# One decoder block for one token: the last rows of the down projection as whole rows, the first keys in one load, and two engines that copy wo's rows

## The chip, the cores and the metric

The kernel runs on one core of a Trainium2 chip. The metric is the device time of one execution in microseconds, the median of several runs. The core has TensorE (matmuls), VectorE, ScalarE, GpSimd and SyncE; each engine works through its own instructions in order and waits for others on semaphores. Data comes from the chip's memory through 16 DMA engines, here nearly all of it by transfers that SyncE issues one after the other on one queue.

## The reference

A block with adaptive layer norm, for a single token of width 640, against a key and value cache of 32 heads x 16384 positions x 128, in bf16:

```python
mod = (_silu(c) @ w_mod).reshape(c.shape[0], 6, 1, -1)
sa, ca, ga, sb, cb, gb = ...
h = _layernorm(x) * (1 + ca) + sa
x = x + ga * attention(h)          # q = h @ wq; softmax(q k^T / sqrt(128)) v for 32 heads; then @ wo
h = _layernorm(x) * (1 + cb) + sb
x = x + gb * ((_silu(h @ w_gate) * (h @ w_up)) @ w_down)      # 640 -> 1728 -> 640
```

Keys and values are 134 MB each; all weights together are 22 MB.

## The kernel before

The 32 heads are worked in 16 pairs. A pair's keys (8.39 MB) are one load into half of the buffer `kring`, its values one load into `vbuf`; the last pair's values go into the other half of `kring`. Each partition holds 256 positions of one of the two heads.

For a pair, VectorE multiplies the keys by the query (mult) and adds halves of the 128 products together (fold), in place, until 16 are left. TensorE adds these 16 with an identity matrix into `S_ps` (R). Then VectorE takes the largest score (pm, nb), ScalarE the exponentials (exp), TensorE the product with the values (pv), and a diagonal is picked out (diag). Pairs 1 to 14 cut the work by columns in `step` (L554, L559, L564, L544), in a loop; pairs 0 and 15 cut it by positions in `score_end` and `reduce_end` (L570, L576, L584), two halves each, by `KCUT`. Pair p's step also does the rest of pair p - 1.

The order of SyncE's loads is written out by hand, and each waits for the buffer that it overwrites. At the start: w_mod, wq, pair 0's keys, pair 1's keys (after mod_mm1, the last reader of w_mod in that half of `kring`), pair 0's values (after the last query matmul, as wq lies in `vbuf`). Then, for each p from 1: the keys of pair p + 1 wait for R of pair p - 1 (`o_R[p - 2]` in `load_k`), the values of pair p for pv of pair p - 1 (`o_pv[p - 1]` in `load_v`). The line of every DMA is L90, that of the helper.

After pair 15's scores the weights of the rest follow on the same queue: wo in two loads after pv14, and w_gate, w_up and w_down in five loads (`DOWN`) after R15. The tail is a chain of small steps: the attention's output A_sb; wo0 and wo28 (L687), 64 matmuls on 32 columns of the array each, four at a time, with 512 and 128 of the 640 outputs in two PSUM banks; the copies of these to `wo_row` on ScalarE (L693); wo_cols (L699); layer norm; gate and up (L724); the gated vector `gu_col` (L754); the down matmuls (L771), 32 columns of the array each and a quarter of the 640 outputs; the product with gb and the sum with x; the store.

F is 1728 = 13 x 128 + 64, so `gu_col` has 14 columns of which the last counts in its upper 64 partitions only. Before the change, the last 64 rows of w_down lie as 128 half rows on 128 partitions, and their factors are spread to match: twice_gu (a matmul with `twice`) repeats each of the 64 factors, gu_half masks them with `even`.

Of the kernel before, what the change touches and what calls it, by code (L numbers as in the profile page):

```python
# [6 lines left out]
BF16 = mybir.dt.bfloat16  # L7
F32 = mybir.dt.float32
ALU = mybir.AluOpType
ACTF = mybir.ActivationFunctionType  # L10
AX = mybir.AxisListType
# [26 lines left out]
class _Plan:  # L38
# [38 lines left out]
    def op(self, eng, fn, deps=(), name="", chan=None):  # L77
        o = _Op(eng, fn, list(deps), name, len(self.ops), self.loop.get(eng), chan)
        o.sig = chan is not None
        self.ops.append(o)  # L80
        return o
# [137 lines left out]
def build(nc, A_x, A_k, A_v, A_wq, A_wo, B_wg, B_wu, B_wd, c_in, w_mod, out):  # L219
    H, S, Dh = A_k.shape[1], A_k.shape[2], A_k.shape[3]  # L220
    D = A_x.shape[2]
    F = B_wg.shape[1]
# [3 lines left out]
    T2 = 2 * S // 128  # L226
# [4 lines left out]
    NF = 13  # L231
# [3 lines left out]
    DOWN = [(0, 0, 4), (1, 0, 4), (2, 0, 4), (3, 0, 1), (None, 0, 0)]  # L235
    FCH = NF + 1
    QW = 32
    QR = 16
    RW = D // 4
# [3 lines left out]
    with es:  # L243
        block = es.enter_context(nc.Block())
        plan = _Plan(nc, es)
        op, dma = plan.op, plan.dma
        POOL, ACT, DVE, PE = "pool", "act", "dve", "pe"

        def sb(name, shape, dtype):
            return es.enter_context(nc.sbuf_tensor(name, list(shape), dtype))  # L250
# [4 lines left out]
        kb = kring[:, 1].rearrange("p t d -> p (t d)")  # L255
# [5 lines left out]
        wu_v = kb[:, KC * F:2 * KC * F].rearrange("p (k n) -> p k n", k=KC)  # L261
        wd0 = 2 * KC * F
        wd_v = kb[:, wd0:wd0 + NF * D].rearrange("p (k n) -> p k n", k=NF)
        wt_v = kb[:, wd0 + NF * D:wd0 + NF * D + D // 2]

        qbc = sb("qbc", [128, NP, 128], BF16)
        PZ = sb("PZ", [128, NCH, 8], BF16)
# [1 line left out]
        ident = sb("ident", [128, 128], BF16)  # L269
# [41 lines left out]
        rg = sb("rg", [128, FCH], F32)  # L311
        sg = sb("sg", [128, FCH], F32)
        gu_col = sb("gu_col", [128, FCH], BF16)
        gu_half = sb("gu_half", [128, 2], BF16)
        even = sb("even", [128, 2], F32)
        twice = sb("twice", [128, 64, 2], BF16)
        o_row = sb("o_row", [128, RW], BF16)
        gb_row = sb("gb_row", [128, RW], F32)
        ind = sb("ind", [128, 1], F32)
# [2 lines left out]
        wo_row = q_f[:, 0:2 * D].bitcast(F32)  # L322
# [11 lines left out]
        wr_ps = [psb[1], psb[6]]  # L334
        cx_ps = psb[4]
        A_ps = psb[6]
        attn_ps = psb[7]
# [22 lines left out]
        o_ident = op(POOL, lambda e: e.affine_select(  # L360
            out=ident[:], in_=ones_bf[:], pattern=[[1, 128]], compare_op=ALU.is_equal,
            fill=0.0, base=0, channel_multiplier=-1), deps=[o_onesb], name="ident")
# [26 lines left out]
        def layernorm_ops(src_f32, src_dep, sum_ap, c0, tag, xc_t, free=None, between=None):  # L389
# [26 lines left out]
            out=sel[:], in_=ident[:].rearrange("p (s r) -> p r s", s=4)[:, 0:8, :], axis=AX.X, op=ALU.add), deps=[o_ident], name="sel")  # L416
        o_msk = op(DVE, lambda e: e.tensor_reduce(
            out=msk[:], in_=ident[:].rearrange("p (j k) -> p j k", k=32), axis=AX.X, op=ALU.add), deps=[o_ident], name="msk")

        def f_e32(e):  # L420
            with nc.allow_low_precision(reason="sum of one 1 and zeros"):
                return e.tensor_reduce(out=e32[:], in_=ident[:].rearrange("p (j k) -> p k j", k=32), axis=AX.X, op=ALU.add)
        o_e32 = op(DVE, f_e32, deps=[o_ident], name="e32")
        o_even = op(DVE, lambda e: e.tensor_reduce(
            out=even[:], in_=ident[:].rearrange("p (j k) -> p k j", k=2), axis=AX.X, op=ALU.add), deps=[o_ident], name="even")
        o_twice = op(DVE, lambda e: e.tensor_copy(out=twice[64:128], in_=ident[64:128, 64:128].unsqueeze(2).broadcast_to([64, 64, 2])), deps=[o_ident], name="twice")
        o_ind = op(DVE, lambda e: e.tensor_copy(out=ind[:], in_=e32[:, 0:1]), deps=[o_e32], name="ind")


# [14 lines left out]
        def pick(half, n, o_m, free):  # L444
# [13 lines left out]
            out=tt1[:], in0=modc[:, KC:2 * KC], scalar=1.0, in1=xn[:], op0=ALU.add, op1=ALU.mult),  # L458
            deps=[o_m0, o_xn], name="t1")
# [11 lines left out]
        for g in range(H // 4):  # L471
            b = g % 2
# [9 lines left out]
            for half in range(2):  # L482
                ps = slice(64 * half, 64 * half + 64)
                ev.append(op(ACT, lambda e, g=g, b=b, half=half, ps=ps: e.activation(
                    out=qbc[ps, 2 * g:2 * g + 2, :],
                    in_=q_ps[b][ps, :].rearrange("p (a h d) -> p a h d", a=2, h=2)[:, :, half, :], func=ACTF.Copy),
                    deps=[o_q[g]], name="qbc%d_%d" % (g, half)))
# [5 lines left out]
        o_R, o_pv, o_exp, o_nb, o_mx, o_acc, o_ot = ([None] * NP for _ in range(7))  # L493
        KCUT = [0, T2 // 2, T2]
# [2 lines left out]

        def load_k(p):
            deps = [o_R[p - 2]] if p >= 2 else ([o_mod[1]] if p == 1 else [])
            cuts = KCUT if p == 0 else [0, T2]  # L500
            d_k[p] = [dma(kring[:, p % 2, a:b], k_src(p)[:, a:b], ("k", p % 2, c), deps=deps, name="dma_k%d_%d" % (p, c))
                      for c, (a, b) in enumerate(zip(cuts, cuts[1:]))]

# [129 lines left out]
        PL = NP - 1  # L633
# [8 lines left out]
        f1 = score_end(PL, 1)  # L642
# [10 lines left out]
        d_wd = []  # L653
        for i, (b, r0, r1) in enumerate(DOWN):
            if b is None:
                dst, src = wt_v, B_wd[NF * 128:F, :].rearrange("q (h n) -> (q h) n", h=2)
            else:
                f0, n, j0 = BLOCKS[b]
                dst, src = wd_v[:, j0 + r0:j0 + r1, :], B_wd[f0:f0 + 128 * n, :].rearrange("(p r) n -> p r n", r=n)[:, r0:r1, :]
            d_wd.append(dma(dst, src, ("wd", i), deps=wdeps, name="dma_wd%d" % i))  # L660
# [4 lines left out]
                 deps=[o_exp[PL], o_rz, o_onesf, o_rstd], name="L")  # L665
# [5 lines left out]
            out=Z[:].rearrange("p (h j) -> p h j", j=4), in0=msk[:].unsqueeze(1).broadcast_to([128, H, 4]),  # L671
            in1=on_f[:].unsqueeze(2).broadcast_to([128, H, 4]), op=ALU.mult), deps=[o_on, o_msk], name="z")
        o_am = op(PE, lambda e: e.matmul(A_ps[:, 0:H], lhsT=Z[:], rhs=e32[:], start=True, stop=True),
                  deps=[o_z, o_e32] + o_qev[-2], name="am")
# [3 lines left out]
            out=Z[:].rearrange("p (j k) -> p j k", k=32), in_=msk[:].unsqueeze(2).broadcast_to([128, 4, 32])), deps=[o_msk, o_am], name="strips")  # L678

        def project(c):  # L680

            def f_wo(e):
                last = None
                for k in range(WCUT[c], WCUT[c + 1]):
                    r = k % 4
                    for ps, a, b in ((wr_ps[0], 0, 512), (wr_ps[1], 512, D)):
                        last = e.matmul(ps[32 * r:32 * r + 32, 0:b - a], lhsT=wide(A_sb[:, k:k + 1]), rhs=wo_v[:, k, a:b],  # L687
                                        start=(k < 4), stop=(k >= H - 4), tile_position=(0, 32 * r))
                return last
            return op(PE, f_wo, deps=[o_as, d_wo[c], o_exp[NP - 2]] + o_qev[-1], name="wo%d" % c)  # L690
        for c in range(len(WCUT) - 1):
            o_p = project(c)
        o_wr = [op(ACT, lambda e, a=a, b=b, ps=ps: e.activation(out=wo_row[:, a:b], in_=ps[:, 0:b - a], func=ACTF.Copy),  # L693
                   deps=[o_p, f1], name="wo_row%d" % a) for ps, a, b in ((wr_ps[0], 0, 512), (wr_ps[1], 512, D))]

        def f_cols(e):
            last = None
# [9 lines left out]
        o_abf = op(DVE, lambda e: e.tensor_copy(out=attn_bf[:], in_=attn_ps[:, 0:KC]), deps=[o_wo], name="attn_bf")  # L707
        o_ga = op(DVE, lambda e: e.tensor_tensor(out=tt2[:], in0=attn_bf[:], in1=ga, op=ALU.mult), deps=[o_abf, o_m0], name="ga_attn")
        o_x1 = op(DVE, lambda e: e.scalar_tensor_tensor(
            out=x1[:], in0=tt2[:], scalar=1.0, in1=x_f32[:], op0=ALU.mult, op1=ALU.add, accum_out=st[:, 4:5]),  # L710
            deps=[o_ga, o_xf], name="x1")
# [18 lines left out]
        def gate0(o_xc1):  # L730
# [6 lines left out]
            deps=[o_xc1, o_rstd1, o_onep_b], name="t2")  # L737
# [14 lines left out]
        o_sg = op(DVE, lambda e: e.tensor_tensor(out=sg[:], in0=g_sb[:], in1=rg[:], op=ALU.mult), deps=[o_rg, o_gs], name="sg")  # L752
        o_x1r = op(ACT, lambda e: e.activation(out=x1_row, in_=xr_ps[:, 0:RW], func=ACTF.Copy), deps=[o_xr], name="x1_row")
        o_gum = op(DVE, lambda e: e.tensor_tensor(out=gu_col[:], in0=u_ps[:, 0:FCH], in1=sg[:], op=ALU.mult), deps=[o_sg, o_u], name="gu")  # L754
        o_tw = op(PE, lambda e: e.matmul(attn_ps[:, 8:9], lhsT=twice[64:128].rearrange("p q h -> p (q h)"), rhs=gu_col[64:128, NF:FCH], start=True, stop=True),
                  deps=[o_gum, o_twice, o_abf], name="twice_gu")
        o_guh = op(DVE, lambda e: e.tensor_tensor(out=gu_half[:], in0=attn_ps[:, 8:9].broadcast_to([128, 2]), in1=even[:], op=ALU.mult),
                   deps=[o_tw, o_even], name="gu_half")

        for i, (b, r0, r1) in enumerate(DOWN):  # L760

            if b is None:
                work = [(gu_half[:, r // 2:r // 2 + 1], wt_v[:, RW * (r % 2):RW * (r % 2) + RW], r) for r in range(4)]
            else:
                j0 = BLOCKS[b][2]
                work = [(gu_col[:, j:j + 1], wd_v[:, j, RW * r:RW * r + RW], r) for j in range(j0 + r0, j0 + r1) for r in range(4)]

            def f_down(e, i=i, work=work):
                last = None
                for at, (col, rows, r) in enumerate(work):  # L770
                    last = e.matmul(f_ps[32 * r:32 * r + 32, 0:RW], lhsT=wide(col), rhs=rows, start=(i == 0 and at < 4),  # L771
                                    stop=(i == len(DOWN) - 1 and at >= len(work) - 4), tile_position=(0, 32 * r))
                return last
            prev = op(PE, f_down, deps=[o_gum if b is not None else o_guh, d_wd[i], o_nb[PL]], name="down%d" % i)
        o_t3 = op(DVE, lambda e: e.tensor_tensor(out=tt_row, in0=f_ps[:, 0:RW], in1=gb_row[:], op=ALU.mult), deps=[prev, o_gb], name="gb_ffn")
        o_or = op(DVE, lambda e: e.tensor_tensor(out=o_row[:], in0=tt_row, in1=x1_row, op=ALU.add), deps=[o_t3, o_x1r], name="o_row")
        o_dst = out[0, 0].rearrange("(r n) -> r n", r=4)
# [51 lines left out]
```

## Time and profile before

| | us |
|---|---|
| median of 3 runs | 680.18 (679.79 to 680.27) |
| profiled execution | 679.98 |
| its span | 678.2 |
| TensorE matmul busy | 366.2 (54%) |
| VectorE busy | 513.0 (76%) |
| ScalarE busy | 46.7 (7%) |
| the load queue's packets, share of 16 engines | 99.2% |
| bytes moved | 290.58 MB, 428 GB/s |

Lines of the profile are given as L and a number of the kernel before. Times in the timeline count from the span's start. In a line of the timeline the first two numbers are start and length, and the bracket at the end is the idle time of that engine just before, with what ended it. "SPq" is SyncE's issue of a transfer. A line of the DMA issues ends with the time from issue to landing. In a group, what follows the bar is the busy time of all its instructions in microseconds, the mean of one in nanoseconds, and the idle time before them.

### The profile page before, as it was taken

How to read it: one execution, taken by the hardware profiler on the slowest of the kernel's cores; microseconds unless marked ns; L12 is line 12 of the kernel's file. 1: busy time of each engine (PE TensorE's matmuls, PEld its weight loads, DVE VectorE, ACT ScalarE, POOL GpSimd, SP SyncE). 2: the span in 40 equal slices, each digit the busy share in tenths (PEclk: the TensorE clock that was granted, in tenths of full speed). 3: DMA queues.
4: the chain of work that ended last, by engine and by line, in shares of the span. 5: the costliest groups of instructions: out<-in, count | busy, mean ns of one | idle time of the engine just before them, and what ended most of it. 6: DMA issues, size and time to landing. Idle time of an engine off the chain costs nothing.

```text
span 678.2 us, 5410 instructions
## 1 busy us (share of the span) xinstructions
PE 366.2 (54%) x2068; PEld 146.5 (22%) x2069; DVE 513.0 (76%) x185; ACT 46.7 (7%) x147; POOL 0.7 (0%) x6
## 2 busy tenths in 40 slices
PE   2522275755728274664818375572818465471677
PEld 1111122221312122221302122121212222130236
DVE  2189997959596896959597795959699695959812
ACT  1120000100000000000000010000000000000011
POOL 0000000000000000000000000000000000000000
PEclk9675565655657565565757555575756556575765
DMA  9999999999999999999999999999999999999997
GB/s 372 442 459 433 433 433 430 433 430 433 437 430 433 433 433 433 433 437 433 433 433 433 437 433 433 433 433 433 433 433 433 433 433 433 433 437 433 434 402 305
DMA packets 6355, 290.58 MB, mean 428 GB/s; under 512 B 714, under 2 KB 972, under 8 KB 1484
## 3 DMA queue, kind: packets, MB, share of 16 engines
q1 hardware_dynamic: 6340, 290.48, 99.2%
q8 instruction: 5, 0.08, 0.0%
q10 hardware_dynamic: 8, 0.00, 0.0%
q14 instruction: 2, 0.02, 0.0%
HBM read 290.47 MB, written 0.00 MB: 428 GB/s over the span
## 4 chain that ended last, share of the span: by engine, by line
DMA 48%; DVE 28%; issue 13%; PE 11%; DVEq 0%; ACT 0%; SPq 0%
DMA kring<-in_A_k_cache_dram 45%; DVE kring L554 10%; PE psb L544 7%; DVE kring L559 6%; DVE kring L570 4%; DVE kring L576 3%; DMA vbuf<-in_A_wo_dram 3%; DVE kring L564 3%; PE psb L518 1%; PE psb L724 1%; PE psb L687 1%; PE psb L584 1%; PE psb L699 0%; PE psb L771 0%; DVE pm L590 0%
## 5 line engine op out<-in xcount | busy, mean ns | idle before, releaser
L554 DVE TENSOR_TENSOR kring<-kring,qbc 128x16384 bf16<-128x16384 bf16 x28 | 243.2, 8687 | 96.2 <-DMA kring<-in_A_k_cache_dram 96.2
L544 PE MATMUL psb<-kring,ident 128*128 x448 | 197.5, 607 | 119.3 <-DVE kring L564 119.3
L559 DVE TENSOR_TENSOR kring<-kring 128x8192 bf16<-128x8192 bf16 x28 | 123.8, 4420 | 0.5
L544 PEld LDWEIGHTS psb<-kring,ident 128*128 128x128 bf16 x448 | 53.9, 120 | 247.1 <-issue 246.0
L518 PE MATMUL psb<-vbuf,PZ 128*8 128x512 bf16 x960 | 82.6, 520 | 0.0
L594 PE MATMUL psb<-d,bd_f 128*128 128x64 f32 x32 | 11.0, 446 | 122.0 <-ACT d L592 122.0
L564 DVE TENSOR_TENSOR kring<-kring 128x4096 bf16<-128x4096 bf16 x28 | 64.0, 2286 | 0.5
L570 DVE TENSOR_TENSOR kring<-kring,qbc 128x16384 bf16<-128x16384 bf16 x4 | 34.8, 8688 | 23.4 <-DMA kring<-in_A_k_cache_dram 23.4
L518 PEld LDWEIGHTS psb<-vbuf,PZ 128*8 128x8 bf16 x960 | 27.0, 109 | 60.2 <-issue 51.5
L584 PE MATMUL psb<-kring,ident 128*128 128x128 bf16 x64 | 14.5, 392 | 40.3 <-DVE kring L576 40.3
L594 PEld LDWEIGHTS psb<-d,bd_f 128*128 128x128 f32 x32 | 8.0, 311 | 124.1 <-DVE pm L590 114.4
L576 DVE TENSOR_TENSOR kring<-kring 128x8192 bf16<-128x8192 bf16 (+2 forms) x12 | 31.7, 2645 | 0.3
L533 PEld LDWEIGHTS psb<-sel,acc_sb 128*128 128x128 f32 x128 | 28.5, 311 | 8.4 <-issue 4.3
L533 PE MATMUL psb<-sel,acc_sb 128*128 128x2 f32 x128 | 25.6, 322 | 1.4 <-ACT acc_sb L524 1.4
L524 ACT ACTIVATE acc_sb<-psb 128x512 f32<-128x512 f32 x16 | 9.6, 597 | 212.0 <-PE psb L518 212.0
L602 ACT ACTIVATE PZ<-psb,nb 64x256 bf16<-64x256 f32 x32 | 15.0, 469 | 64.8 <-DVE nb L598 64.6
L584 PEld LDWEIGHTS psb<-kring,ident 128*128 128x128 bf16 x64 | 7.4, 122 | 46.7 <-DVE kring L576 41.6
L592 ACT ACTIVATE d<-negid,pm 128x64 f32<-128x64 f32 x16 | 5.6, 348 | 153.9 <-DVE pm L590 153.9
L477 PE MATMUL psb<-vbuf,h_col 128*128 128x512 bf16 x39 | 11.2, 461 | 8.3 <-DMA vbuf<-in_A_wq_dram 8.3
L537 ACT ACTIVATE OT_sb<-psb 128x2 f32 (+1 forms) x16 | 2.8, 172 | 151.3 <-PE psb L533 151.3
L590 DVE TENSOR_REDUCE pm<-psb 128x1 f32<-128x256 f32 x16 | 6.7, 418 | 3.7 <-PE psb L584 3.7
L477 PEld LDWEIGHTS psb<-vbuf,h_col 128*128 128x128 bf16 x40 | 4.3, 116 | 15.6 <-DMA vbuf<-in_A_wq_dram 8.8
(104 smaller groups left out, 80.4 us busy)
## 6 DMA issues: line engine op xcount, KB each, us to landing
kring<-in_A_k_cache_dram SPq DMA_DIRECT2D x2, 4096.0 KB, 40.3
vbuf<-in_A_wq_dram SPq DMA_DIRECT2D x1, 5120.0 KB, 25.9
kring<-in_w_mod_dram SPq DMA_DIRECT2D x1, 4800.0 KB, 14.2
vbuf<-in_A_wo_dram SPq DMA_DIRECT2D x1, 4480.0 KB, 23.0
kring<-in_B_w_gate_dram SPq DMA_DIRECT2D x1, 2160.0 KB, 18.7
kring<-in_B_w_up_dram SPq DMA_DIRECT2D x1, 2160.0 KB, 23.5
kring<-in_B_w_down_dram SPq DMA_DIRECT2D x3, 640.0 KB, 25.7
vbuf<-in_A_wo_dram SPq DMA_DIRECT2D x1, 640.0 KB, 24.2
```

What stands on the lines that cost most here:

```text
L477: last = e.matmul(q_ps[b][:, 0:512], lhsT=h_col[:, k:k + 1].broadcast_to([128, 128]), rhs=wq_v[:, k, g * 512:(g + 1) * 512], start=(k == 0 ...
L518: last = e.matmul(acc_ps[32 * s:32 * s + 8, :], lhsT=PZ[:, j, :], rhs=v_at(p)[:, 4 * j:4 * j + 4, :].rearrange("p t d -> p (t d)"), start= ...
L533: last = e.matmul(OT_ps[:, 0:2], lhsT=acc_sb[:, 128 * i:128 * (i + 1)], rhs=sel[:, i:8:4], start=(i == 0), stop=(i == 3))
L544: last = e.matmul(S_ps[:, 0:T2], lhsT=ident[:], rhs=kring[:, bass.ds(plan.slot(p), 1), :, d].rearrange("p o t -> p (o t)"), start=(d == 0) ...
L554: return e.tensor_tensor(out=kv4, in0=kv4, in1=q4, op=ALU.mult)
L559: o_f = op(DVE, lambda e: e.tensor_tensor(out=kv4[:, :, 0], in0=kv4[:, :, 0], in1=kv4[:, :, 1], op=ALU.add), deps=[o_m], name="fold%d_%d" ...
L564: return op(DVE, lambda e: e.tensor_tensor(out=lo[:, :, 0:QR], in0=lo[:, :, 0:QR], in1=lo[:, :, QR:QW], op=ALU.add), deps=[o_f], name="fol ...
L570: o = op(DVE, lambda e: e.tensor_tensor(out=kv, in0=kv, in1=qbc[:, p, :].unsqueeze(1).broadcast_to([128, KCUT[c + 1] - KCUT[c], 128]), op= ...
L576: o = op(DVE, lambda e, w=w: e.tensor_tensor(out=kv[:, :, 0:w], in0=kv[:, :, 0:w], in1=kv[:, :, w:2 * w], op=ALU.add), deps=[o], name="fol ...
L584: last = e.matmul(S_ps[:, KCUT[c]:KCUT[c + 1]], lhsT=ident[:], rhs=kring[:, p % 2, KCUT[c]:KCUT[c + 1], d], start=(d == 0), stop=(d == 15))
L594: o_mx[p] = op(PE, lambda e: e.matmul(mx_ps[:, 0:64], lhsT=bd_f[:], rhs=d2[:], start=True, stop=True), deps=[o_d2, o_bd1, o_bd2, o_nb[p - ...
L602: o_exp[p] = op(ACT, lambda e, half=half, ps=ps: e.activation(out=PZ[ps, :, 4 * half:4 * half + 4], in_=S_ps[ps, 0:T2].rearrange("p (c i) ...
```

## The change

It has three parts. The last 64 rows of w_down are loaded as 64 whole rows on partitions 64 to 127, and their four matmuls use these 64 rows of the array with `gu_col` as it is; twice_gu, gu_half and the setup of `twice` and `even` go. Pair 0's keys come in one load rather than two. wo's 640 outputs are split 320 and 320 between two PSUM banks, ScalarE copies the one and VectorE the other.

```diff
-        wt_v = kb[:, wd0 + NF * D:wd0 + NF * D + D // 2]
+        wt_v = kb[64:128, wd0 + NF * D:wd0 + NF * D + D]
...
-        o_even = op(DVE, lambda e: e.tensor_reduce(
-            out=even[:], in_=ident[:].rearrange("p (j k) -> p k j", k=2), axis=AX.X, op=ALU.add), deps=[o_ident], name="even")
-        o_twice = op(DVE, lambda e: e.tensor_copy(out=twice[64:128], in_=ident[64:128, 64:128].unsqueeze(2).broadcast_to([64, 64, 2])), deps=[o_ident], name="twice")
...
         def load_k(p):
             deps = [o_R[p - 2]] if p >= 2 else ([o_mod[1]] if p == 1 else [])
-            cuts = KCUT if p == 0 else [0, T2]
+            cuts = [0, T2]
...
             if b is None:
-                dst, src = wt_v, B_wd[NF * 128:F, :].rearrange("q (h n) -> (q h) n", h=2)
+                dst, src = wt_v, B_wd[NF * 128:F, :]
...
-                    for ps, a, b in ((wr_ps[0], 0, 512), (wr_ps[1], 512, D)):
+                    for ps, a, b in ((wr_ps[0], 0, D // 2), (wr_ps[1], D // 2, D)):
...
-        o_wr = [op(ACT, lambda e, a=a, b=b, ps=ps: e.activation(out=wo_row[:, a:b], in_=ps[:, 0:b - a], func=ACTF.Copy),
-                   deps=[o_p, f1], name="wo_row%d" % a) for ps, a, b in ((wr_ps[0], 0, 512), (wr_ps[1], 512, D))]
+        o_wr = [op(ACT, lambda e: e.activation(out=wo_row[:, 0:D // 2], in_=wr_ps[0][:, 0:D // 2], func=ACTF.Copy), deps=[o_p, f1], name="wo_row0"),
+                op(DVE, lambda e: e.tensor_copy(out=wo_row[:, D // 2:D], in_=wr_ps[1][:, 0:D // 2]), deps=[o_p, f1], name="wo_row1")]
...
-        o_tw = op(PE, lambda e: e.matmul(attn_ps[:, 8:9], lhsT=twice[64:128].rearrange("p q h -> p (q h)"), rhs=gu_col[64:128, NF:FCH], start=True, stop=True),
-                  deps=[o_gum, o_twice, o_abf], name="twice_gu")
-        o_guh = op(DVE, lambda e: e.tensor_tensor(out=gu_half[:], in0=attn_ps[:, 8:9].broadcast_to([128, 2]), in1=even[:], op=ALU.mult),
-                   deps=[o_tw, o_even], name="gu_half")
...
-                work = [(gu_half[:, r // 2:r // 2 + 1], wt_v[:, RW * (r % 2):RW * (r % 2) + RW], r) for r in range(4)]
+                work = [(gu_col[64:128, NF:FCH], wt_v[:, RW * r:RW * r + RW], r) for r in range(4)]
...
-                                    stop=(i == len(DOWN) - 1 and at >= len(work) - 4), tile_position=(0, 32 * r))
+                                    stop=(i == len(DOWN) - 1 and at >= len(work) - 4), tile_position=(64 if b is None else 0, 32 * r))
...
-            prev = op(PE, f_down, deps=[o_gum if b is not None else o_guh, d_wd[i], o_nb[PL]], name="down%d" % i)
+            prev = op(PE, f_down, deps=[o_gum, d_wd[i], o_nb[PL]], name="down%d" % i)
```

More of the change, by code (lines that the diff above doesn't have):

```diff
@@ L313, in build @@
         gu_col = sb("gu_col", [128, FCH], BF16)
-        gu_half = sb("gu_half", [128, 2], BF16)
-        even = sb("even", [128, 2], F32)
-        twice = sb("twice", [128, 64, 2], BF16)
         o_row = sb("o_row", [128, RW], BF16)
@@ L766, in build, with f_down @@
                 work = [(gu_col[:, j:j + 1], wd_v[:, j, RW * r:RW * r + RW], r) for j in range(j0 + r0, j0 + r1) for r in range(4)]
-            def f_down(e, i=i, work=work):
+            def f_down(e, i=i, b=b, work=work):
                 last = None
```

## The prediction

> **What bounds the kernel now.** The page first. The load queue is busy in every slice, and the chain that ended last is almost half loads of keys.
>
> ```profile
> DMA  9999999999999999999999999999999999999997
> GB/s 372 442 459 433 433 433 430 433 430 433 437 430 433 433 433 433 433 437 433 433 433 433 437 433 433 433 433 433 433 433 433 433 433 433 433 437 433 434 402 305
> q1 hardware_dynamic: 6340, 290.48, 99.2%
> DMA 48%; DVE 28%; issue 13%; PE 11%; DVEq 0%; ACT 0%; SPq 0%
> ```
>
> So the end is set by when SyncE's one queue has moved its bytes, plus a short tail after the last weights. VectorE at 76% has room in the loop, though perhaps not at the start, where the change makes it wait. Hence the timeline of the first 110 us, of which these lines matter (start, length, engine, line, tile, idle before it and what ended that):
>
> ```profile
> 36.89 8.69 DVE L570 TENSOR_TENSOR kring<-kring,qbc 128x16384 bf16<-128x16384 bf16 x1 [16.02 <-DMA kring<-in_A_k_cache_dram]
> ...
> 73.99 0.33 SPq L90 DMA_DIRECT2D kring<-in_A_k_cache_dram  x1
> ...
> 93.29 5.84 PE L518 MATMUL psb<-vbuf,PZ 128*8 128x512 bf16 x64
> ...
> 99.18 0.33 SPq L90 DMA_DIRECT2D vbuf<-in_A_v_cache_dram  x1
> ...
> 105.77 8.69 DVE L554 TENSOR_TENSOR kring<-kring,qbc 128x16384 bf16<-128x16384 bf16 x1 [4.50 <-DMA kring<-in_A_k_cache_dram]
> ```
>
> The first product of keys starts at 36.89, the moment the first half of pair 0's keys lands. From there VectorE runs without a gap to 101.27, and everything SyncE may issue hangs on that run: the keys of pair 2 (73.99, after R0_1), the values of pair 1 (99.18, after pv0), the keys of pair 3 (108.50). The first idle VectorE sees afterwards is the 4.50 us before 105.77.
>
> Next, when each load lands, from the DMA issues in narrow windows (issue to landing, us). In order: pair 0's second half, pair 1's keys, pair 0's values, pair 2's keys, pair 1's values:
>
> ```profile
> kring<-in_A_k_cache_dram SPq DMA_DIRECT2D x1, 4096.0 KB, 45.4
> kring<-in_A_k_cache_dram SPq DMA_DIRECT2D x1, 47.7
> vbuf<-in_A_v_cache_dram SPq DMA_DIRECT2D x1, 47.5
> kring<-in_A_k_cache_dram SPq DMA_DIRECT2D x1, 31.8
> vbuf<-in_A_v_cache_dram SPq DMA_DIRECT2D x1, 25.9
> ```
>
> With their issues at about 2.1, 19.3, 38.87, 73.99 and 99.18 they land at 47.5, 67.0, 86.4, 105.8 and 125.1: one per 19.4 us, the 8.39 MB of a load at 433 GB/s, back to back. The reserve is what is issued ahead. Pair 1's values are issued 6.6 us before the load in front of them lands (105.8 - 99.18); that is the thinnest cover of the start.
>
> **The first keys in one load.** `score_end(0, 0)` now waits for the whole 8.39 MB. Its last byte sits in the queue where the second half's did, so it lands at 47.5 instead of 36.8, and mult0_0 starts at about 47.6: 10.7 us late. If the second half's own 10.7 us (9.7 is its share by bytes) had 1 us of unevenness between the 16 engines in it, 9.7. As VectorE has no gap from there to 101.27, its whole run moves by that. What each issue then meets:
>
> Pair 2's keys go out at 84.7 and the load ahead of them lands at 86.4, so the queue is just about kept full there; a start-up of a micro-second or two could cost some tenths, which the next item swallows. Pair 1's values go out at 99.18 + 10.7 = 109.9, while the queue has run empty at 105.8. Here it stands still. pv0 is TensorE work at the granted clock (0.50 to 1.00 at 96 to 100 us); its 5.84 us is 4.93 to 6.12 in the pairs after it, mean about 5.5, so I take 0.3 off: 109.6.
>
> The trace of before shows no big load meeting an empty queue except the first of all. w_mod is issued at 0.80 and lands 14.2 later; its 4.92 MB need 11.35 at 433 GB/s, so 2.85 us go to starting and landing, and some 0.9 of them are a pause at 3 to 4 us (DMA busy share 0.1) that may belong to the start of the program alone. From below, the last store: 0.33 us of issue and 0.8 until the final wait is released, 1.1. I take 2.4, between 2.85 and 1.95 without the pause, as w_mod is the nearest in size; 1.1 and 2.85 stay as ends.
>
> The values of pair 1 then land at 109.6 + 2.4 + 19.4 = 131.4 instead of 125.1: **6.3 us late**. Nothing behind gives it back, as the queue has no spare rate (433 GB/s in every slice). Nothing behind adds to it either: VectorE starts pair 2 at 101.27 + 10.7 = 112.0, 6.2 late; pair 2's values are issued at 134.04 + 6.2 = 140.2 and pair 4's keys at 144.07 + 6.2 = 150.3, both before pair 3's keys land at 131.4 + 19.4 = 150.8. From there VectorE waits for keys again, as it did before (7.42 us of idle ahead of pair 15), and the rest is the old schedule 6.3 us later. Ends: 9.7 late, pv0 0.9 shorter, 1.1 to start gives 99.18 + 9.7 - 0.9 + 1.1 + 19.4 - 125.1 = 3.4; 10.7, pv0 0.3 longer, 2.85 gives 7.3. One issue of 0.4 us on SyncE goes, at 2 us, where k1 behind it waits for mod_mm1 until 19.3 anyway: nothing.
>
> **wo's rows on two engines.** Before, from the timeline of the tail and its groups by form:
>
> ```profile
> L693 ACT ACTIVATE qbc<-psb 128x512 f32<-128x512 f32 x1 | 0.6, 598 | 4.6 <-PE psb L687 4.6
> L693 ACT ACTIVATE qbc<-psb 128x128 f32<-128x128 f32 x1 | 0.3, 271 | 0.0
> L687 PE MATMUL psb<-vbuf,A_sb 128*32 128x512 bf16 x32 | 4.4, 631 | 0.3 <-ACT A_sb L675 0.3
> ```
>
> Both copies stand on the path: 0.77 us for the two. After, ScalarE's 320 columns cost about 0.43 (between 271 ns for 128 and 598 for 512) and VectorE's at most 0.48 (its 320-column product of L446 at 19.36, which also reads PSUM). They run side by side: 0.77 - 0.48 = 0.29 us less. The 64 matmuls stream the same 640 columns per head: nothing. On VectorE the zeroing of g_ps and u_ps (0.08 and 0.07) now queues behind the copy, but gate0, which needs it, comes 4 us later.
>
> **Down's last rows.** twice_gu (0.18) is ahead of the down matmuls on TensorE; the first of them starts 0.11 us after it (673.72, 673.83), so 0.11 leaves the path. gu_half (0.16 on VectorE) lay beside the other 52 matmuls: nothing. The two setup reductions even and twice, 0.5 us at 11.85, stood in VectorE's wait for w_mod: nothing. The last load is the same 80 KB in half as many pieces: between 0 and 0.2 us.
>
> Together the tail's engines run 0.40 us earlier, but the loads do not. w_down's third load is issued at 648.0 and lands after 26.7, at 674.7; its matmuls begin some 32 x 0.031 us behind 673.83, at 674.8. So only 0.1 of the 0.40 is free before TensorE meets the weights, and I take **-0.1**, with ends -0.4 (if the landing is rounded the wrong way or moves) and +0.2.
>
> The last four matmuls now use 64 rows of the array where those before use 128. The one such step in the trace, from twice_gu (64 rows) to the down matmuls, let the next weights load begin 0.11 us after twice_gu, before its 0.18 had ended, so I add nothing. The Trainium skill (TensorEngine Tiling (Array Packing), Tiling Modes, Key Properties) says on the contrary that changing the tiling mode drains TensorE. By it the last four would wait for the 0.34 us of the matmuls before them, some 0.3 us more, and the sum by it is 686.5; only a trace of after can show it.
>
> **Sum.** The profiled execution took 679.98 (span 678.2 and 1.78 around it; the median of the three runs, 680.18, is 0.20 above). 679.98 + 6.3 - 0.1 = **686.2 us**.
>
> **Rivals.** (a) The whole delay passes through: 679.98 + 10.7 - 0.1 = 690.6. For it speaks the chain of waits, which goes from 36.89 along VectorE and TensorE to 108.50. Against it: the 36 us after 108.50 are spent behind two queued loads, so a later issue of pair 3's keys costs nothing until the queue is empty. Chance 0.06.
>
> (b) Not slower: the cover of pair 1's values holds. This decides at one place, the landing at 105.8: if the values are issued before 105.8 - 2.4 = 103.4, the queue never empties and only the tail is left, 679.98 - 0.1 to - 0.4, 679.6 to 679.9. That asks for a delay under 4.2 us, so for the whole first keys at 41 us, 8.39 MB in the 14 us after w_q's landing at 27.2, 600 GB/s; the queue showed 433. A faster pv0 alone gives 0.9. Chance 0.04.
>
> (c) Each load carries a price of its own, and one load fewer saves it. The halves then cost more than their bytes, and the merged keys land sooner. Taking the 1.0 us that the second half took over its share, doubled for both halves, the delay is 8.7 and the time 684.2. Against: w_q to the first half is 27.2 to 36.8, 9.7 us for exactly half of a 19.4 load, no price in it. Chance 0.10. The Trainium skill (DMA: Bandwidth & Descriptors, Anatomy of one DMA) gives each DMA, for the GpSimd path, a fixed cost of about 2.0 us beside its bytes, and advises large transfers; in a full queue this trace doesn't show it, and as the start-up on an empty queue it would make the sum 685.8.
>
> (d) The change does not do what it says: excluded for the keys, as both `score_end` calls index the only load there is.
>
> **How the numbers follow.** The forecast has 0.80, (a) 0.06, (b) 0.04, (c) 0.10. The range runs from the low ends, 679.98 + 3.4 - 0.4 = 683.0, to the high ones, 679.98 + 7.3 + 0.2 = 687.5, and takes in (c). A measurement of this kernel tells about 0.2%, 1.4 us, from no change; (b) gains less than that, so its 0.04 goes to same, but 0.01 to faster. Slower: 0.95.
>
> **What would show it.** Right: mult0_0 near 47.6; SyncE's issues at about 84.7, 109.6 and 119; one dip of the GB/s near 106 to 112 and none elsewhere; the keys of pair 15 landing near 615 instead of 608.87; 0.48 us from the last wo matmul to wo_cols. Wrong: mult0_0 before 42, no dip, a second dip near 140 to 150, or the tail after pair 15's keys changing by more than half a micro-second.

## The result, and the profile after

The changed kernel takes 688.16 us (687.21 to 688.59, 4 runs) against 680.06 (679.79 to 680.27, 4 runs): ratio 1.0117, 95% interval 1.0101 to 1.0133. The profiled execution took 688.03, its span 686.2. Slower was forecast, but by 6.2 us of the profiled execution, up to 7.5 at the range's end; it was 8.05.

Of the page of the changed kernel, the lines that answer to those of before:

```profile
DMA  9999897999999999999999999999999999999997
GB/s 392 445 425 428 371 428 307 428 428 428 428 459 447 432 432 428 428 432 428 428 428 455 447 432 432 432 428 428 432 428 428 428 458 447 428 432 432 425 404 298
q1 hardware_dynamic: 6132, 290.48, 98.3%
DMA 45%; DVE 34%; issue 13%; PE 8%; SPq 0%; DVEq 0%; ACT 0%
```

The queue that never paused has two dents, in the fifth slice (69 to 86 us; pair 2's keys are issued 1.8 us ahead of the landing before them, 86.7, and land at 107.0, 20.3 us after it and not 19.4) and the deeper one in the seventh (103 to 120 us); VectorE's share of the chain rises from 28% to 34%. The timeline of the changed kernel shows what moved:

```profile
47.75 8.69 DVE L564 TENSOR_TENSOR kring<-kring,qbc 128x16384 bf16<-128x16384 bf16 x1 [27.20 <-DMA kring<-in_A_k_cache_dram]
...
84.86 0.33 SPq L90 DMA_DIRECT2D kring<-in_A_k_cache_dram  x1
...
104.15 5.42 PE L512 MATMUL psb<-vbuf,PZ 128*8 128x512 bf16 x64
...
109.62 0.33 SPq L90 DMA_DIRECT2D vbuf<-in_A_v_cache_dram  x1
...
112.05 8.68 DVE L548 TENSOR_TENSOR kring<-kring,qbc 128x16384 bf16<-128x16384 bf16 x1
...
119.36 0.33 SPq L90 DMA_DIRECT2D kring<-in_A_k_cache_dram  x1
```

The first product starts 10.86 us late, and pair 1's values are issued 10.44 us late. VectorE meets pair 2's keys at 112.05 without having waited, where before it waited 4.50 us. The windows there (PE, PEld, DVE, ACT, POOL busy; granted clock; share of the 16 DMA engines; GB/s):

```profile
104.00:106.00 2.00, 2.00 (x21) 0.66 (x24) 1.97 (x2) 0.00 (x0) 0.00 (x0) 0.50 0.08 33
106.00:108.00 2.00, 2.00 (x28) 0.65 (x20) 2.00 (x1) 0.00 (x0) 0.00 (x0) 0.54 0.00 0
108.00:110.00 2.00, 1.57 (x32) 0.46 (x20) 1.97 (x2) 0.37 (x1) 0.00 (x0) 1.00 0.00 0
110.00:112.00 2.00, 0.00 (x0) 0.00 (x0) 2.00 (x1) 0.23 (x1) 0.00 (x0) 1.00 1.53 524
```

The last two columns count a packet in the window in which it begins, with its whole time and all of its bytes, so a share can exceed 1. A row of 64 KB is one packet and takes 2.42 us. By the single packets in the trace, the 16 engines end pair 2's keys at 105.7 to 106.7 and begin pair 1's values at 110.6 to 111.1: each engine stands for some 4.6 us. The issues in narrow windows, pair 2's keys, pair 1's values and pair 3's keys:

```profile
kring<-in_A_k_cache_dram SPq DMA_DIRECT2D x1, 22.1
vbuf<-in_A_v_cache_dram SPq DMA_DIRECT2D x1, 23.0
kring<-in_A_k_cache_dram SPq DMA_DIRECT2D x1, 32.6
```

Pair 1's values land at 109.62 + 23.0 = 132.6 instead of 125.1, 7.5 us late; pair 3's keys at 152.0, 19.4 later as ever. The first product of pair 15 then starts at 616.41 instead of 608.87, 7.54 late: nothing was given back or added in 460 us. From there to the end of the span it is 69.8 us, where it was 69.3. In the tail of the changed kernel:

```profile
665.87 2.37 PE L681 MATMUL psb<-vbuf,A_sb 128*32 128x320 bf16 x64 [0.40 <-DMA vbuf<-in_A_wo_dram]
668.30 0.44 ACT L687 ACTIVATE qbc<-psb 128x320 f32<-128x320 f32 x1 [2.59 <-PE psb L681]
668.30 0.49 DVE L688 COPY qbc<-psb 128x320 f32<-128x320 f32 x1 [2.56 <-PE psb L681]
...
677.65 2.43 PE L718 MATMUL psb<-h_col,kring 128*128 128x1 bf16 x70 [1.66 <-DMA kring<-in_B_w_up_dram]
...
680.41 0.94 PEld L760 LDWEIGHTS psb<-kring,gu_col 128*32 128x32 bf16 x32 [0.42 <-DVE gu_col L748]
...
682.73 0.54 PEld L760 LDWEIGHTS psb<-kring,gu_col 128*32 128x32 bf16 x20 [1.38 <-DMA kring<-in_B_w_down_dram]
...
683.51 0.11 PEld L760 LDWEIGHTS psb<-kring,gu_col 64*32 64x32 bf16 x4 [0.25 <-DMA kring<-in_B_w_down_dram]
```

The engines are early here: the wo matmuls take 2.37 us instead of 4.47, at a granted clock of 1.00 instead of 0.50. They spend it waiting for w_up (1.66) and for w_down's third load (1.38 on the weights loads). Ahead of the last four weights loads is a gap of 0.25 that the kernel before does not have.

### The profile page after: what moved, and what is told of

Read it like the earlier page. It is cut to its first block, busy times and chain, and to the rows that moved or that the text cites. A ratio compares the mean times of both kernels' runs of the same rounds, so it can differ in the third digit from the quotient of the medians.

```text
span 686.2 us, 5405 instructions
## 1 busy us (share of the span) xinstructions
PE 361.6 (53%) x2067; PEld 145.2 (21%) x2068; DVE 512.9 (75%) x183; ACT 46.4 (7%) x146; POOL 0.7 (0%) x6
## 4 chain that ended last, share of the span: by engine, by line
DMA 45%; DVE 34%; issue 13%; PE 8%; SPq 0%; DVEq 0%; ACT 0%
DMA kring<-in_A_k_cache_dram 41%; DVE kring L548 13%; DVE kring L553 8%; PE psb L538 7%; DVE kring L564 5%; DVE kring L570 5%; DMA kring<-in_B_w_down_dram 4%; DVE kring L558 3%; PE psb L578 1%; SPq L90 0%; DVE pm L584 0%; DVE nb L592 0%; PE psb L527 0%; PE psb L760 0%; DVEq L191 0%
## 5 line engine op out<-in xcount | busy, mean ns | idle before, releaser
L512 PE MATMUL psb<-vbuf,PZ 128*8 128x512 bf16 x960 | 80.2, 508 | 0.0
L588 PEld LDWEIGHTS psb<-d,bd_f 128*128 128x128 f32 x32 | 8.0, 312 | 120.7 <-DVE pm L584 111.1
```

The costliest lines, as they stand in the source:

```text
L512: last = e.matmul(acc_ps[32 * s:32 * s + 8, :], lhsT=PZ[:, j, :], rhs=v_at(p)[:, 4 * j:4 * j + 4, :].rearrange("p t d -> p (t d)"), start= ...
L588: o_mx[p] = op(PE, lambda e: e.matmul(mx_ps[:, 0:64], lhsT=bd_f[:], rhs=d2[:], start=True, stop=True), deps=[o_d2, o_bd1, o_bd2, o_nb[p - ...
```

## The experiments

Theory Q: one load makes VectorE late, so pair 1's values are issued late and the queue runs empty. Theory L: the tail is set by the landing of the last weights.

**The keys alone** (`keys_only`: the kernel before with this edit).

```diff
-            cuts = KCUT if p == 0 else [0, T2]
+            cuts = [0, T2]
```

> The kernel before with pair 0's keys in one load, nothing else. Theory Q (the queue runs empty because pair 1's values are issued some 10.5 us later): mult0_0 near 47.7, pair 1's values issued near 109.6 and landing 23.0 later, pair 15's keys landing 7.5 us later than before (near 616.4), and the time 680.1 + 7.5 = 687.6. With the tail of before, the rest from that landing to the end of the span is 69.3 as before. Rival W (the whole delay passes through to the end): 690.7. Rival P (one load fewer saves a price, the rest of the slowdown is the tail's): 684 to 686.

687.28 us, ratio 1.0105 (1.0090 to 1.0121). In its profile the first product starts at 47.36, pair 1's values are issued at 109.07 and land 22.9 later, and pair 15's first product starts at 615.81, 6.9 us late; from there the span has 69.3 us, as before. So this edit has nearly all of the slowdown, and none of it is in the tail. W would be 690.7, P 686 at most.

**Is it the lateness or the load?** (`keys_less_work`: `keys_only` with 8.0 us less work for VectorE, as it leaves out the three folds of pair 0's first half.)

```diff
-            for i, w in enumerate((64, 32, 16)):
+            for i, w in enumerate((64, 32, 16) if (p, c) != (0, 0) else ()):
```

> keys_only with the three folds of pair 0's first half left out (8.0 us of VectorE's work ahead of pair 1's values; that half's scores are then not those of the reference). Pair 0's keys still come in one load. Theory Q: VectorE is 2.7 us late instead of 10.7, pair 1's values are issued near 101.9, before the 105.8 at which the queue would run empty, they land at 125.1 as in the kernel before, and the time is that of before, 680.0 (679.6 to 681). If the single load itself costs something, or its landing, the time stays near 687.

680.37 us, ratio 1.0009 (0.9999 to 1.0018), though the keys still come in one load. The timeline:

```profile
101.75 0.33 SPq L90 DMA_DIRECT2D vbuf<-in_A_v_cache_dram  x1
...
105.69 8.69 DVE L554 TENSOR_TENSOR kring<-kring,qbc 128x16384 bf16<-128x16384 bf16 x1 [1.76 <-DMA kring<-in_A_k_cache_dram]
```

VectorE waits for keys again. The load is not what costs; the late issue behind it is. Its profiled execution took 681.71, at the upper end of its runs (679.90 to 682.81), and has two loads that land 20.1 and 20.3 us after the one ahead where 19.4 is usual. In the first, pair 1's values, the packets show four of the 16 engines without work from about 103.4 to 105.2 and later, though the issue is 3.9 us ahead of the landing before it (105.7); why these four is not known. In the second, a packet of 8 KB of the queue that the page lists as instruction begins at 149.64 and the last engine ends 0.9 us further behind the others than in the load ahead.

**How much lateness the queue bears** (`keys_5of8`, `keys_3of4`, `keys_7of8`: the kernel before, only the place of the first cut).

```diff
-            cuts = KCUT if p == 0 else [0, T2]
+            cuts = [0, 3 * T2 // 4, T2] if p == 0 else [0, T2]
```

> The kernel before with the first keys cut at three quarters instead of a half: two loads, and the first product waits for three quarters. Theory Q: mult0_0 near 42.4, 5.5 us late; pair 1's values issued near 104.5, 1.3 us before the load ahead of them lands. If a load needs its 3.5 us from issue even with the queue not yet empty, they land at 104.5 + 22.9 = 127.4, 2.3 us late, and the time is 682.3. If the 3.5 us is mostly paid on an empty queue, less: 680.5 to 681.5. Rival W (every us of VectorE's delay passes through): 685.5.

> The kernel before with the first keys cut at five eighths. Theory Q with the rule from the earlier runs (a load lands at the later of 19.4 us after the one ahead of it and 22.9 to 23.2 us after its own issue): mult0_0 near 40.0, 3.1 late (2.7 to 3.3); pair 1's values issued near 102.2 and landing at 125.1 to 125.4; pair 15's keys at most 0.3 us late; time 680.0 to 680.6. Rival W: 683.2.

> The kernel before with the first keys cut at seven eighths. Theory Q with the same rule: mult0_0 near 45.0, 8.1 late; pair 1's values issued near 107.2 and landing at 130.1 to 130.4, 5.0 to 5.3 late; time 685.1 to 685.5. Rival W: 688.2. With 3.5 us paid only once the queue is empty, and less just before, three quarters would have been cheaper than the line through one and seven eighths; with the rule, the times lie on one line of 1 us per us of delay from a delay of 2.7 on.

| kernel | first product | pair 1's values issued | landing | issue to landing | pair 15's keys, late | median us |
|---|---|---|---|---|---|---|
| before (half) | 36.89 | 99.18 | 125.1 | 25.9 | 0 | 680.02 to 680.11 |
| `keys_5of8` | 38.99 | 100.97 | 125.3 | 24.3 | 0.2 | 680.15 |
| `keys_3of4` | 42.75 | 104.89 | 128.1 | 23.2 | 3.0 | 683.26 |
| `keys_7of8` | 45.20 | 107.84 | 131.0 | 23.2 | 5.9 | 684.85 |
| `keys_only` | 47.36 | 109.07 | 132.0 | 22.9 | 6.9 | 687.28 |

The ratios of the three are 1.0008 (0.9999 to 1.0017), 1.0045 (1.0030 to 1.0061) and 1.0067 (1.0052 to 1.0083). Once late, a load lands about 23 us after its own issue, 3.5 to 3.8 beyond its 19.4, and that lateness reaches pair 15 to the tenth. The medians scatter around this by up to 1 us: `keys_7of8` has 684.85, its profiled execution 685.86.

Three quarters is the case in point: the issue at 104.89 is still 0.6 us ahead of the landing before it (105.5), and 3.0 us are lost all the same. From the windows of `keys_3of4`:

```profile
102.80:105.80 3.00, 2.04 (x32) 0.61 (x24) 2.97 (x2) 0.60 (x1) 0.00 (x0) 0.90 0.00 0
105.80:106.90 1.10, 0.00 (x0) 0.00 (x0) 1.10 (x1) 0.00 (x0) 0.00 (x0) 1.00 2.88 953
```

No row begins between 102.8 and 105.8. By the packets, fifteen of the 16 engines end pair 2's keys at 103.2 to 103.9, the last one at 105.2, and pair 1's values begin at 105.85. So a landing is not the moment at which the queue runs empty: at the issue fifteen engines had been without work for 1.0 to 1.7 us. In the kernel before, too, the landing at 105.7 comes 2.2 us after the median engine has ended its rows; only there the next rows were already waiting. An issue has to lead the landing ahead of it by the 3.5 us. The delays themselves came out up to 1 us off the expectation (first product 38.99, not 40.0); why was not looked into.

**What the 3.5 us are** (`keys_halved_values`: `keys_only` with the values in two loads).

```diff
-            cuts = VCUT if p == NP - 1 else [0, T2]
+            cuts = VCUT if p == NP - 1 else [0, T2 // 2, T2]
```

> keys_only with every pair's values, but the last's, in two loads of half the positions (32 KB rows instead of 64 KB), one after the other, and pv in two halves to match. It asks where the 3.5 us of a load on an empty queue come from. Theory S (the 16 engines start in step, each with one whole row, and the start costs by the size of the rows): pair 1's values land 21 to 22 us after the first issue instead of 22.9, and the time is 685.8 to 686.6. Rival F (a fixed time to start): 22.9 and 687.3. If pieces cost in the full queue, all landings spread wider than 19.4 per pair and it is slower than keys_only.

688.10 us, ratio 1.0119 (1.0104 to 1.0135). The first half of pair 1's values, from the issues in a narrow window, 4.19 MB or 9.7 us of bytes:

```profile
vbuf<-in_A_v_cache_dram SPq DMA_DIRECT2D x1, 4096.0 KB, 13.1
```

13.1 - 9.7 = 3.4, and the second half lands 22.8 us after the first issue. Half the row and half the load change next to nothing, and theory S falls.

The packets show what the price is made of. Each engine has eight rows of a load. In the changed kernel, from the last rows of pair 2's keys to the second rows of pair 1's values:

```profile
103.20:104.30 1.10, 1.10 (x7) 0.22 (x9) 1.10 (x1) 0.00 (x0) 0.00 (x0) 0.50 2.20 953
104.30:110.50 6.20, 5.27 (x64) 1.66 (x56) 6.13 (x3) 0.60 (x1) 0.00 (x0) 0.72 0.00 0
110.50:111.20 0.70, 0.00 (x0) 0.00 (x0) 0.70 (x1) 0.00 (x0) 0.00 (x0) 1.00 4.37 1498
111.20:113.60 2.40, 1.33 (x4) 0.47 (x5) 2.40 (x2) 0.00 (x0) 0.00 (x0) 1.00 0.00 0
113.60:114.20 0.60, 0.60 (x3) 0.17 (x2) 0.60 (x1) 0.00 (x0) 0.00 (x0) 1.00 4.03 1748
```

The values are issued at 109.62, and their first rows begin at 110.58, 1.0 us later. These take 3.06 us in the mean, 0.6 more than the 2.42 of a row in the stream. On one engine a packet of 16 KB of the queue that the page lists as instruction comes in between at 116.19 (0.89 us, and the row behind it 0.55 longer); that engine ends at 132.1, 1.4 us behind the median of the 16. The landing follows 0.5 us later. 1.0 + 0.6 + 1.4 + 0.5 = 3.5, of the 3.6 (23.0 - 19.4). In the halved values the same parts are 1.0, 0.5, 1.4 and 0.5.

**wo's rows alone** (`wo_only`: the kernel before with the two wo edits of the change).

```diff
-                    for ps, a, b in ((wr_ps[0], 0, 512), (wr_ps[1], 512, D)):
+                    for ps, a, b in ((wr_ps[0], 0, D // 2), (wr_ps[1], D // 2, D)):
...
-        o_wr = [op(ACT, lambda e, a=a, b=b, ps=ps: e.activation(out=wo_row[:, a:b], in_=ps[:, 0:b - a], func=ACTF.Copy),
-                   deps=[o_p, f1], name="wo_row%d" % a) for ps, a, b in ((wr_ps[0], 0, 512), (wr_ps[1], 512, D))]
+        o_wr = [op(ACT, lambda e: e.activation(out=wo_row[:, 0:D // 2], in_=wr_ps[0][:, 0:D // 2], func=ACTF.Copy), deps=[o_p, f1], name="wo_row0"),
+                op(DVE, lambda e: e.tensor_copy(out=wo_row[:, D // 2:D], in_=wr_ps[1][:, 0:D // 2]), deps=[o_p, f1], name="wo_row1")]
```

> The kernel before with wo's 640 outputs split 320 and 320 and copied by ScalarE and VectorE, nothing else. Theory L (the tail ends with the weights' landing): the two copies take 0.49 instead of 0.77 us, but TensorE then waits for w_up or for w_down's third load, so the time changes by 0.0 to -0.15: 679.9 to 680.1. Rival E (the engines set the tail): -0.3, 679.8.

680.08 us, ratio 1.0000 (0.9991 to 1.0009). gu_col is computed 0.65 us earlier (672.84 instead of 673.49; the wo matmuls took 3.64 us here instead of 4.47, so the copies are only a part of it), and TensorE waits for w_down's third load instead:

```profile
674.82 0.54 PEld L771 LDWEIGHTS psb<-kring,gu_col 128*32 128x32 bf16 x20 [0.71 <-DMA kring<-in_B_w_down_dram]
```

From pair 15's first product to the end of the span are 69.29 us, where before had 69.33.

**The whole rows alone, and both edits of the tail** (`down_only`: the kernel before with the down edits of the change; `wo_down`: the changed kernel with this).

```diff
-            cuts = [0, T2]
+            cuts = KCUT if p == 0 else [0, T2]
```

> The kernel before with the last 64 rows of w_down as whole rows on the upper 64 partitions, nothing else. Theory L: the end is the landing of w_down's last loads and does not gain from the 0.11 us of twice_gu. If the 0.5 us by which w_down's third load landed later in the changed kernel (66.3 instead of 65.8 us after pair 15's keys) comes from this load, it shows here: 680.4 to 680.7. If it is chance between the 16 engines, 679.9 to 680.1 on average, with that landing spread by half a micro-second between profiles. Rival E: -0.1. A drain of TensorE ahead of the last four matmuls would show as a gap of 0.2 to 0.3 us between the third-last and the last group of weights loads, with the last load landed.

> The changed kernel with pair 0's keys in two loads again: both edits of the tail, not the keys. Theory L: no gain beyond 0.15, and if the whole rows delay the landing, up to 0.5 us slower: 679.9 to 680.6. Rival E: 679.98 - 0.40 = 679.6. Rival P (the slowdown sits in the tail): 683 or more.

680.46 us, ratio 1.0005 (0.9996 to 1.0014), and 680.39, ratio 1.0005 (0.9996 to 1.0014). As times neither is told from no change, but the traces differ in the same two places. The tail from pair 15's first product is 69.7 and 69.8 us, where the three with half rows (before, `wo_only`, `keys_only`) have 69.3. w_down's third load lands 66.2 us after that product in both (66.3 in the changed kernel); with half rows it is 65.8 to 65.9. And both have the gap of 0.25.

**The place of the whole rows** (`down_third`, `down_second`: `wo_down` with another order of the five loads and their matmuls).

```diff
-    DOWN = [(0, 0, 4), (1, 0, 4), (2, 0, 4), (3, 0, 1), (None, 0, 0)]
+    DOWN = [(0, 0, 4), (1, 0, 4), (None, 0, 0), (2, 0, 4), (3, 0, 1)]      # down_third
+    DOWN = [(0, 0, 4), (None, 0, 0), (1, 0, 4), (2, 0, 4), (3, 0, 1)]      # down_second
```

> wo_down with the last 64 rows' load and its four matmuls third of the five instead of last. If the 0.25 us gap ahead of these matmuls is TensorE changing from 128 to 64 rows of the array, it now lies in the wait for the fourth load and leaves the path: the last group starts right behind, -0.25 against wo_down. If w_down's 640 KB load after it still lands at 66.2 after pair 15's keys, the whole rows' load delays what is near it and the sum is 680.15; if it lands at 65.9 or (80 KB later) 66.0, 679.9. If the gap is a wait for the load, it stays at the end.

> wo_down with the last 64 rows' load and its four matmuls second of the five, so that they and the first load have landed before gu_col is ready. If the 0.25 us gap is TensorE's change from 128 to 64 rows of the array, it stands between the first 16 and these four matmuls though nothing waits for a load. If it was the load's wait, there is no gap. The load's effect on its neighbours, if it is the 64 rows': the first 640 KB load or the second lands 0.4 to 0.6 us later than in the kernel before (62.6 and 64.3 after pair 15's keys) and all after it 0.4 to 0.8 later; time 680.3 to 680.6.

680.58 us, ratio 1.0008 (0.9999 to 1.0017), and 680.72, ratio 1.0011 (1.0002 to 1.0020). `down_second` settles the gap. Weights loads of its timeline:

```profile
672.74 0.41 PEld L760 LDWEIGHTS psb<-kring,gu_col 128*32 128x32 bf16 x16 [0.42 <-DVE gu_col L748]
673.40 0.11 PEld L760 LDWEIGHTS psb<-kring,gu_col 64*32 64x32 bf16 x4 [0.25 <-issue]
```

Both loads had landed (63.3 and 63.7 us after pair 15's first product at 608.73, so by 672.5), nothing is waited for, and the 0.25 stands there all the same, where 128 rows change to 64. The rest of the +0.45 moves along with the load: in `down_third` w_down's second load lands at 64.9 instead of 64.3, in `down_second` the first at 63.3 instead of 62.6, so in both the load just ahead of the whole rows is late. Both orders are no better than the last place, as all loads behind are then late too (the last at 67.1).

**The half of the partitions** (`down_lower`: the same 64 rows on the lower half, where gu_col holds the factors of other rows).

```diff
-        wt_v = kb[64:128, wd0 + NF * D:wd0 + NF * D + D]
+        wt_v = kb[0:64, wd0 + NF * D:wd0 + NF * D + D]
```

> wo_down with the last 64 whole rows loaded to the lower 64 partitions and multiplied there with the lower half of gu_col's last column (so with the wrong 64 factors). If a load on half of the partitions delays the loads around it whichever half it is: w_down's third load lands 66.2 after pair 15's keys, time 680.4. If it is the upper half: 65.9, and 680.1 plus the change of rows, 680.3.

680.21 us, ratio 1.0003 (0.9994 to 1.0012); the third load lands at 66.0, between the 66.2 and the 65.8 to 65.9, and the gap of 0.25 is there, so it goes with the 64 rows and not with the half. A tenth or two of one profile decide nothing: why the whole rows delay their neighbours stays open.

## Why the prediction was wrong, and where it was right

**The lateness: right.** The whole load lands where the second half did; mult0_0 was put at 47.6 (47.75), SyncE's issues at 84.7, 109.6 and about 119 (84.86, 109.62, 119.36), TensorE's share of it at 0.3 less (5.42 for 5.84). The place of the loss, the reserve of 6.6 us, and that all behind it moves as a block, held to the tenth. One sign failed: a single dip was forecast, and there are two. At the first, pair 2's keys were put at just about in time; they land 0.9 us beyond 19.4, and pair 1's later issue swallows it, as forecast.

**The price of starting: the step that failed.** It was 2.85 in the row of w_mod, the only big load on an empty queue. I took 0.9 us of it for a pause that belongs to the program's start and settled on 2.4, with 2.85 as the upper end. There was no pause: a window counts a packet where it begins, and the 16 engines' first rows of w_mod begin at 1.83 to 2.63 and end at 3.85 to 4.80. They begin 1.0 us after the issue and take up to 2.8 us where the rows behind take 1.42, so they are the start itself. The price is 3.6 in the changed kernel (23.0 - 19.4) and 3.4 to 3.8 in the others: 1.2 us of the miss of 1.8 between the profiled 688.03 and the 686.2. Discounting the only row there was made it worse, and that one row was no upper bound: w_mod's rows had no instruction packet among them, the 1.4 us of pair 1's values. With it rival (b)'s point was wrong too: the values must be out by 105.8 - 3.6 = 102.2, not 103.4; `keys_5of8` (100.97) and `keys_3of4` (104.89) lie on either side, and `keys_less_work` (101.75) had already lost 0.7 in its profiled execution.

**The tail: the other failure, 0.56 us** (+0.46 instead of -0.1). That the 0.40 us of the engines would be lost to the landing of w_down's third load was right (`wo_only`: 0.04 gained), though wo_cols starts 0.67 us after the last wo matmul, not 0.48 (before: 0.88). The load in half as many pieces was put at between 0 and 0.2 us; in the five kernels that have the whole rows on the upper half, a load ahead of them lands 0.3 to 0.6 later, of a cause that stays open. And the change of rows was put at nothing, by a row in which one single matmul is ahead of it, twice_gu after a wait. The other view given there was the better one: the page TensorEngine Tiling (Array Packing) of the Trainium skill, Tiling Modes, Key Properties, says that a change of tiling mode drains TensorE, and `down_second` shows 0.25 us for it, close to the 0.3 reckoned by it.

**Rivals.** (a), the whole delay, would have been 690.6; pair 15 was 7.5 late, not 10.9. (b) did not happen; `keys_5of8` shows that the cover holds, to 0.2 us, for a delay of 2.1. (c), a price per load that merging saves: in the full queue there is one, but a small one. The halved values take 19.43 us per pair from one landing to the next, the single loads 19.35, so a further load costs 0.08. Over the 13 pairs from pair 2 to 14 that is 1.0, and with the 0.3 by which pair 1's values land later it is the 1.25 us by which that kernel's keys of pair 15 come later than in `keys_only` (617.06 and 615.81). The 2.0 us that (c) reckoned for the merged keys are not there: they land at 47.7, as the second half did.

Together: 679.98 + 7.54 + 0.46 = 687.98, beside the measured 688.03.

## What to carry to other kernels

Where one queue is the bound, look for the transfer that is issued with the least lead over the landing ahead of it: the lead, less the time from an issue to the landing beyond the bytes, is how late its releasers may be, and past that point every microsecond shows at the end. Leave some room there, as `keys_less_work` lost 0.7 us with a lead of 3.9. And do not take a landing for the moment at which the queue runs empty: it is that of the slowest engine, and in the kernel before the median engine was done 2.2 us earlier. Take the start of a transfer from a row undiscounted, and if there is only one row, leave room above it. In a tail that waits for weights, faster engines gain nothing, and here the last load's shape and a change of tile height cost more than the instructions saved.

## What the runs showed of the hardware that was not expected

- A load of 8.39 MB whose lead was used up landed 22.9 to 23.2 us after its issue, though its bytes take 19.4 in the stream; with half of that load it was 3.4 us over. Issued 0.6 us ahead of the landing before it, it still paid in full, as fifteen of the 16 engines had ended their rows 1.0 us or more before the issue.
- An instruction packet of 16 KB held up one engine by 1.4 us, and with it the landing of the load whose rows it came between.
- A load of 64 rows on the upper half of the partitions made a 640 KB load ahead of it in the same queue land 0.3 to 0.6 us later, in all five kernels that have it.
- The 64 wo matmuls took 2.37 us in one kernel and 4.47 in another, by the granted clock at that moment (1.00 and 0.50), and the time of the kernel did not notice.
